# Output pieces sent in turn from SyncE and GpSimd, with a buffer for each, and the first piece scaled in column halves

## The chip, the cores and the metric

The kernel runs on one core of a Trainium2 chip. The metric is the device time of one execution in microseconds. The profile is of one execution; its times count from the start of its span.

## The reference

Two layers follow each other. The first is a linear-attention recurrence over r, k and v (batch 4, heads 8, sequence 768, head size 48). Its output, read as x with 3072 rows and 384 columns, goes into a soft mixture of experts with 32 slots (8 experts, 4 slots each):

```python
logits = x @ phi                         # 3072 x 32
d = softmax(logits over rows)            # dispatch
slot_input = d.T @ x                     # 32 x 384
for e in range(E):
    slot_out[e] = relu(slot_input[e] @ w1[e]) @ w2[e]
c = softmax(logits over slots)           # combine
return (c @ slot_out).astype(np.float32) # 3072 x 384, 4.72 MB
```

Only the last line matters here: every output row is a weighted sum of the 32 rows of slot_out, divided by the sum of its weights.

## The kernel before, in words

The order of the instructions on every engine is written out by hand. The kernel has three parts.

The attention part (to about 97 us of the span) works in twelve steps of 256 rows, two chunks of 128 each. It loads r, k and v through SyncE and forms x and the exponentials of the logits. The exponentials are turned round into `LexpT` (slots on the partitions, one column a row), and their sums over the slots are inverted into `rsum_r`, one value for each row. While it runs, GpSimd scales r and k and issues the loads of all the weights, `w_all`, `w_h` and `w_tail` (`w1_load`, `w2_load`), which convert from float32 to bf16 on the way. An early load, `phi_f` (L116), is GpSimd's too.

The expert part runs from about 97 to 110 us. It ends in two PSUM tiles `sr_p[0]` and `sr_p[1]` of 192 columns (HD) each, which hold slot_out, repeated for four groups of 32 slots. DVE (L726) scales the first into columns 0 to 191 of `so_r`, and ACT (L727) the second into columns 192 to 383.

The output part (L729 to L751) is what the change rewrites. The output is cut into twelve pieces, i = 0 to 11, of 256 rows: 128 partitions with two rows (j = 0, 1) of 384 float32 values, which lie one behind the other in HBM, so that a partition sends 3072 bytes. For each j, two matmuls of 384 columns (q2 = 0, 1) put 64 rows each into one PSUM tile `o_p`. Then j = 0 is scaled by `rsum_r` on DVE (L745) and j = 1 on ACT (L747), both into the SBUF tile `o_s`. Piece 0 leaves in two DMAs, one for each j (L749); every other piece leaves in one DMA of 384 KB (L751). All of them are issued by SyncE. The pool `ob` has six `o_s` buffers, so piece 6 can't be scaled before piece 0 has landed. The pool `out_ps` has four names of `o_p` with two buffers each[...].

At the end of the program (L777) each engine drains, SyncE waits for the DMAs, and the engines meet.

Of the kernel before, what the change touches and what calls it, by code (L numbers as in the profile page):

```python
# [11 lines left out]
def kernel(  # L12
# [12 lines left out]
    nc = tc.nc  # L25
# [3 lines left out]
    Nn, Dm = out.shape  # L29
    assert Nn == B * S and Dm == H * D  # L30
    ES = moe_phi.shape[1]
# [6 lines left out]
    f32 = mybir.dt.float32  # L38
    bf = mybir.dt.bfloat16
    AF = mybir.ActivationFunctionType  # L40
    ALU = mybir.AluOpType

    P = 128
# [9 lines left out]
    HF = P // J  # L53
# [45 lines left out]
    for par in range(2):  # L99
        nc.scalar.dma_start(out=w_pd[par * 64:par * 64 + D, :],  # L100
                            in_=w.rearrange("(q a) d -> a d q", a=2)[par])
# [76 lines left out]
    LexpT = cst.tile([P, nG, P], bf, name="LexpT")  # L178
# [31 lines left out]
    with tc.tile_pool(name="wk", bufs=2) as wk, \  # L210
# [23 lines left out]
        for Wt, ex in ((W_k, ex_k), (W_n, ex_n)):  # L234
            for j in range(J):
                nc.scalar.activation(out=Wt[:, j, :, :].rearrange("p h d -> p (h d)"), in_=lw_p[:], func=AF.Exp,
                                     scale=ex[:, j:j + 1])
# [380 lines left out]
    with tc.tile_pool(name="ffn", bufs=2) as ffn, \  # L618
# [84 lines left out]
        so_r = cst.tile([P, Dm], bf, name="so_r")  # L703
        HD = Dm // 2
# [22 lines left out]
        nc.scalar.activation(out=so_r[:, HD:Dm], in_=sr_p[1][:], func=AF.Copy, scale=csum_c[:])  # L727

    out_ap = out.rearrange("(i p j) m -> i p j m", p=P, j=J)  # L729
    with tc.tile_pool(name="ob", bufs=6) as ob, \  # L730
         tc.tile_pool(name="out_ps", bufs=2, space=bass.MemoryType.PSUM) as out_ps:
        for i in range(nS):
            g, qh = divmod(i, 2)
            o_s = ob.tile([P, J, Dm], f32, name="o_s")
            for j in range(J):
                o_p = out_ps.tile([P, Dm], f32, name=f"o_p{2 * qh + j}")
                for q2 in range(2):
                    q = 2 * qh + q2
                    nc.tensor.matmul(o_p[q2 * HF:(q2 + 1) * HF, :],
                                     LexpT[q * ES:(q + 1) * ES, g, j * HF:(j + 1) * HF],  # L740
                                     so_r[q * ES:(q + 1) * ES, :],
                                     tile_position=(q * ES, q2 * HF), skip_group_check=True)
                sc_col = rsum_r[:, g * G + 2 * j + qh:g * G + 2 * j + qh + 1]
                if j == 0:
                    nc.vector.tensor_scalar_mul(o_s[:, j, :], o_p[:], sc_col)  # L745
                else:
                    nc.scalar.activation(out=o_s[:, j, :], in_=o_p[:], func=AF.Copy, scale=sc_col)  # L747
                if i == 0:
                    nc.sync.dma_start(out=out_ap[i][:, j, :], in_=o_s[:, j, :])  # L749
            if i > 0:  # L750
                nc.sync.dma_start(out=out_ap[i], in_=o_s[:])  # L751


# [28 lines left out]
```

## Time and profile before

| | |
|---|---|
| time, median of 5 runs | 129.59 us (128.57 to 133.58) |
| the profiled execution's own time | 128.61 us |
| its span | 126.4 us, granted TensorE clock 0.91 |
| busy in the span | PE 96.8 us, DVE 92.4, ACT 79.1, POOL 77.7 |
| output DMAs | 11 of 384 KB, median 4.6 us from issue to landing, and 2 of 192 KB, 2.9 us |
| HBM | 39.38 MB read, 4.72 MB written |

The span goes from the first to the last instruction; the rest of an execution's time lies around it. A busy share is an average over the three parts; what a change in the output part is worth has to be read in the last 17 us.

### The profile page before, as it was taken

The numbers are of one execution on the slowest core, as the hardware profiler recorded it, in microseconds if no ns is written. First come the engines' busy times: TensorE is split into PE (matmuls) and PEld (weight loads), VectorE is DVE, ScalarE is ACT, GpSimd is POOL, SyncE is SP. The second block draws the span as 40 slices with busy tenths as digits, with TensorE's granted clock in tenths as the row PEclk, the third lists the DMA queues.
The fourth block names the chain that finished last, engine by engine and source line by source line (L and its number), as shares of the span: only waits on it lengthen the run. The fifth ranks groups of instructions, "written<-read, shape, count | busy, mean of one in ns | idle before, by whom it ended". The sixth has DMA issues, their size and how long they took to land.

```text
span 126.4 us, 4177 instructions
## 1 busy us (share of the span) xinstructions
PE 96.8 (77%) x1779; PEld 69.6 (55%) x1779; DVE 92.4 (73%) x180; ACT 79.1 (63%) x143; POOL 77.7 (61%) x70
## 2 busy tenths in 40 slices
PE   3994799968697888269698959979699999794100
PEld 3483578756566666157485738767576566521000
DVE  5499989999999999275999995999963421284700
ACT  5869495969697966278688877779422320283600
POOL 6008999899998899998599999997420000000000
PEclk9999999999999999756999995899999999995555
DMA  3999999999999999999999999999999999069992
GB/s 77 302 324 325 325 328 267 325 212 232 282 296 290 229 260 256 344 252 301 236 255 257 242 213 220 218 215 214 217 218 213 216 201 180 16 249 365 395 399 93
DMA packets 23544, 31.78 MB, mean 251 GB/s; under 512 B 10451, under 2 KB 18133, under 8 KB 23525
## 3 DMA queue, kind: packets, MB, share of 16 engines
q0 software_dynamic: 4816, 12.63, 51.3%
q1 hardware_dynamic: 18288, 18.88, 47.6%
q8 instruction: 14, 0.23, 0.7%
q10 hardware_dynamic: 420, 0.00, 0.2%
q14 instruction: 6, 0.04, 0.1%
HBM read 39.38 MB, written 4.72 MB: 349 GB/s over the span
## 4 chain that ended last, share of the span: by engine, by line
DMA 45%; PE 14%; POOL 12%; SPq 8%; ACT 6%; DVE 6%; issue 4%; POOLq 0%; DVEq 0%; ACTq 0%
DMA w_tail<-in_moe_w_dram 15%; DMA rkv<-in_v_dram 14%; DMA w_h<-in_moe_w_dram 10%; SPq L83 8%; DMA out_dram<-o_s 6%; POOL kk L256 3%; PE t_p L312 3%; POOL rkv L257 3%; POOL rr L254 3%; PE aat_p L331 2%; PE s_p L382 2%; DVE at_s L343 2%; ACT t_kk L319 2%; DVE rpun L294 2%; PE lw_p L232 1%
## 5 line engine op out<-in xcount | busy, mean ns | idle before, releaser
L343 DVE TENSOR_TENSOR at_s<-aat_p,mask 128x512 bf16<-128x512 f32 x47 | 30.2, 684 | 4.2 <-PE aat_p L331 3.9
L254 POOL TENSOR_TENSOR rr<-rkv,W_n 128x768 bf16<-128x768 f32 x11 | 20.1, 1825 | 10.2 <-DMA rkv<-in_r_dram 10.1
L257 POOL TENSOR_TENSOR rkv<-rkv,u_rep 128x768 f32<-128x768 f32 x11 | 19.9, 1810 | 0.9
L256 POOL TENSOR_TENSOR kk<-rkv,W_k 128x768 bf16<-128x768 f32 x11 | 20.0, 1817 | 0.1
L331 PE MATMUL aat_p<-t_rr,t_kk 64*64 64x128 bf16 x376 | 12.0, 243 | 9.2 <-ACT t_kk L319 6.6
L277 ACT COPY rpun<-rkv 128x384 f32<-128x384 f32 x23 | 11.3, 492 | 9.6 <-PE rpun L491 7.5
L331 PEld LDWEIGHTS <-t_kk 64*64 64x64 bf16 x384 | 8.4, 119 | 12.4 <-ACT t_kk L319 8.7
L301 DVE TENSOR_TENSOR dv<-v_bf,rpun 128x768 bf16<-128x768 bf16 x12 | 11.4, 954 | 3.6 <-ACT v_bf L264 2.6
L319 ACT COPY t_kk<-t_p 128x1024 bf16<-128x1024 bf16 x12 | 12.2, 1013 | 1.4 <-PE t_p L312 1.4
L283 DVE TENSOR_TENSOR rkv<-rkv,rpun 128x384 f32<-128x384 f32 x23 | 12.6, 548 | 0.1
L294 DVE TENSOR_REDUCE rpun<-rkv 128x16 f32<-128x768 f32 x12 | 11.5, 961 | 0.4
L264 ACT CAST v_bf<-rkv 128x768 bf16<-128x768 f32 x12 | 10.0, 831 | 2.9 <-DMA rkv<-in_v_dram 2.9
L319 ACT COPY t_rr<-t_p 128x1024 bf16<-128x1024 bf16 x11 | 11.2, 1016 | 0.5 <-PE t_p L312 0.3
L382 PE MATMUL s_p<-v_bf,kk 64*128 64x96 bf16 x160 | 11.4, 218 | 0.0
L391 DVE TENSOR_TENSOR st<-s_p,wm 128x384 bf16<-128x384 f32 x20 | 10.9, 547 | 0.5 <-PE s_p L382 0.3
L433 ACT COPY xt_s<-xl_p 128x768 bf16<-128x768 bf16 x11 | 8.8, 798 | 3.4 <-PE xl_p L431 3.3
L382 PEld LDWEIGHTS <-kk 64*128 64x128 bf16 x160 | 8.3, 102 | 3.8 <-issue 3.7
L745 DVE TENSOR_SCALAR o_s<-o_p,rsum_r 128x384 f32<-128x384 f32 x12 | 7.0, 615 | 3.7 <-DMA out_dram<-o_s 3.2
L412 ACT CAST x_t<-y_p 128x384 bf16<-128x384 f32 x22 | 9.6, 494 | 0.0
L312 PE MATMUL t_p<-ident,kk 128*128 128x128 bf16 x96 | 8.3, 234 | 1.2 <-ACT Lexp L478 0.6
L488 PE MATMUL rpun<-Lexp,x_t 128*128 128x32 bf16 x66 | 5.2, 180 | 5.2 <-DVE dv L301 5.1
L747 ACT ACTIVATE o_s<-o_p,rsum_r 128x384 f32<-128x384 f32 x12 | 6.4, 584 | 4.1 <-DMA out_dram<-o_s 3.5
(130 smaller groups left out, 186.3 us busy)
## 6 DMA issues: line engine op xcount, KB each, us to landing
w_all<-in_moe_w_dram POOLq DMA_DIRECT2D x8, 768.0 KB, 11.7
out_dram<-o_s SPq DMA_DIRECT2D x11, 384.0 KB, 4.6
w_h<-in_moe_w_dram POOLq DMA_DIRECT2D x4, 768.0 KB, 12.4
w_tail<-in_moe_w_dram POOLq DMA_DIRECT2D x3, 768.0 KB, 18.9
rkv<-in_k_dram SPq DMA_DIRECT2D x3, 384.0 KB, 4.5
rkv<-in_r_dram SPq DMA_DIRECT2D x3, 384.0 KB, 4.9
rkv<-in_v_dram SPq DMA_DIRECT2D x3, 384.0 KB, 5.0
w_tail<-in_moe_w_dram POOLq DMA_DIRECT2D x4, 192.0 KB, 20.1
```

The lines of the kernel that those rows point to most:

```text
L254: nc.gpsimd.tensor_mul(rr[:, :, :, 0:D], r_l, W_n[:])
L256: nc.gpsimd.tensor_mul(kk[:, :, :, 0:D], k_l, W_k[:])
L257: nc.gpsimd.tensor_mul(ku, ku, u_b)
L277: nc.scalar.copy(rp, loads[n][0][:, j, :, :])
L283: nc.vector.tensor_mul(s["ku"][:, j, :, :], s["ku"][:, j, :, :], s["rps"][j])
L294: nc.vector.tensor_reduce(d, s["ku"], axis=mybir.AxisListType.X, op=ALU.add)
L301: nc.vector.tensor_mul(dv[:], s["v"][:], d[:, :, :, None].to_broadcast([P, J, H, D]))
L312: nc.tensor.transpose(t_p[:, q, :, j, :], s[nm][:, j, 2 * q:2 * q + 2, :].rearrange("p h d -> p (h d)"), ident[:])
L319: nc.scalar.copy(t_s[:], s.pop("p_" + nm)[:])
L331: nc.tensor.matmul(at_p[a][g * HF:(g + 1) * HF, q, :], kT[sl, q, g, j, :], rT[sl, q, g, :, :].rearrange("p j c -> p (j c)"), start=True, s ...
L343: nc.vector.tensor_mul(s["at"][:, a, j, :, :], at_p[a][:], mask[:, j, None, :].to_broadcast([P, nP, P]))
L382: nc.tensor.matmul(s_p[:, q * D2:(q + 1) * D2], s["kk"][sl, j, 2 * q:2 * q + 2, :].rearrange("p h d -> p (h d)"), s["v"][sl, j, 2 * q:2 * ...
```

## The change

It touches the output loop alone.

- The pool `ob` has twelve buffers, one for each piece.
- The DMAs of pieces 2, 4, 6, 8 and 10 are issued by SyncE as before; those of pieces 1, 3, 5, 7, 9 and 11 by GpSimd. Of piece 0, the row j = 0 is issued by SyncE and j = 1 by GpSimd.
- Piece 0 is computed in column halves: for each j, columns 0 to 191 go through one `o_p` and DVE, columns 192 to 383 through another `o_p` and ACT. Before, DVE scaled the whole of j = 0 and ACT the whole of j = 1.

```diff
-    with tc.tile_pool(name="ob", bufs=6) as ob, \
+    with tc.tile_pool(name="ob", bufs=12) as ob, \
          tc.tile_pool(name="out_ps", bufs=2, space=bass.MemoryType.PSUM) as out_ps:
         for i in range(nS):
             g, qh = divmod(i, 2)
             o_s = ob.tile([P, J, Dm], f32, name="o_s")
+            put = nc.sync.dma_start if i % 2 == 0 else nc.gpsimd.dma_start
             for j in range(J):
-                o_p = out_ps.tile([P, Dm], f32, name=f"o_p{2 * qh + j}")
-                for q2 in range(2):
-                    q = 2 * qh + q2
-                    nc.tensor.matmul(o_p[q2 * HF:(q2 + 1) * HF, :],
-                                     LexpT[q * ES:(q + 1) * ES, g, j * HF:(j + 1) * HF],
-                                     so_r[q * ES:(q + 1) * ES, :],
-                                     tile_position=(q * ES, q2 * HF), skip_group_check=True)
                 sc_col = rsum_r[:, g * G + 2 * j + qh:g * G + 2 * j + qh + 1]
-                if j == 0:
-                    nc.vector.tensor_scalar_mul(o_s[:, j, :], o_p[:], sc_col)
-                else:
-                    nc.scalar.activation(out=o_s[:, j, :], in_=o_p[:], func=AF.Copy, scale=sc_col)
+                parts = ((0, HD), (HD, Dm)) if i == 0 else ((0, Dm),)
+                for c, (d0, d1) in enumerate(parts):
+                    o_p = out_ps.tile([P, Dm], f32, name=f"o_p{2 * j + c if i == 0 else 2 * qh + j}")
+                    for q2 in range(2):
+                        q = 2 * qh + q2
+                        nc.tensor.matmul(o_p[q2 * HF:(q2 + 1) * HF, d0:d1],
+                                         LexpT[q * ES:(q + 1) * ES, g, j * HF:(j + 1) * HF],
+                                         so_r[q * ES:(q + 1) * ES, d0:d1],
+                                         tile_position=(q * ES, q2 * HF), skip_group_check=True)
+                    if (c if i == 0 else j) == 0:
+                        nc.vector.tensor_scalar_mul(o_s[:, j, d0:d1], o_p[:, d0:d1], sc_col)
+                    else:
+                        nc.scalar.activation(out=o_s[:, j, d0:d1], in_=o_p[:, d0:d1], func=AF.Copy, scale=sc_col)
                 if i == 0:
-                    nc.sync.dma_start(out=out_ap[i][:, j, :], in_=o_s[:, j, :])
+                    (nc.sync if j == 0 else nc.gpsimd).dma_start(out=out_ap[i][:, j, :], in_=o_s[:, j, :])
             if i > 0:
-                nc.sync.dma_start(out=out_ap[i], in_=o_s[:])
+                put(out=out_ap[i], in_=o_s[:])
```

## The prediction

> **What bounds the kernel now.** I read the page first (the 40 slices and the chain that ended last), then the chain in order of time, the windows of the last 16 us, each SyncE issue there, the DMA view in narrow windows, and the closing instructions. The change touches nothing before 109.6 us of the span, so the question is only what sets the time from there to 126.4 us.
>
> The chain of waits, its last steps (start, length, what):
>
> ```profile
> 109.26 0.43 ACT so_r L727
> 109.73 0.61 PE o_p L739 x8
> 110.34 0.90 ACT o_s L747 x2
> 111.24 3.67 DMA out_dram<-o_s
> 115.09 4.45 DMA out_dram<-o_s
> ```
>
> The chain runs through output DMAs. The windows tell whether that is their latency or their volume (length; busy us of PE, PEld, DVE, ACT, POOL; granted clock; DMA share; GB/s):
>
> ```profile
> 111.40:111.60 0.20, 0.20 (x4) 0.14 (x4) 0.20 (x1) 0.20 (x1) 0.00 (x0) 1.00 0.00 0
> 111.60:112.00 0.40, 0.39 (x6) 0.10 (x4) 0.40 (x2) 0.40 (x2) 0.00 (x0) 1.00 0.74 261
> 112.00:114.60 2.60, 1.94 (x16) 0.43 (x16) 1.42 (x3) 1.26 (x3) 0.00 (x0) 0.86 1.04 386
> 114.70:115.00 0.30, 0.00 (x0) 0.00 (x0) 0.00 (x0) 0.00 (x0) 0.00 (x0) 0.50 0.21 72
> 115.00:124.00 9.00, 1.70 (x8) 0.36 (x7) 3.71 (x6) 3.48 (x6) 0.00 (x0) 0.50 1.01 394
> 124.00:125.20 1.20, 0.00 (x0) 0.00 (x0) 0.00 (x0) 0.00 (x0) 0.00 (x0) 0.50 0.06 23
> ```
>
> It is volume. From about 111.66 us the 16 DMA engines are full at 386 to 394 GB/s until 124.0. 4.72 MB at 394 GB/s take 11.97 us; 12.3 pass. The only hole is 114.7 to 115.0, worth 0.3 x (1 - 0.21) = 0.24 us. After 124.0 a share of 0.06 is one engine of sixteen: a straggler that works to nearly 125.2. POOL is idle here.
>
> What made the hole? Two SyncE issues, from narrow timelines:
>
> ```profile
> 110.82 0.37 SPq L749 DMA_DIRECT2D out_dram<-o_s  x1
> 112.81 1.69 SPq L751 DMA_DIRECT2D out_dram<-o_s  x1
> ```
>
> DVE and ACT had filled all six buffers by 113.42, without a wait. SyncE held one issue for 1.69 us, to 114.50, and piece 3's bytes came about 0.5 us later. So the hole is an issue held back on SyncE's queue, not a missing buffer. The waits of L745 and L747 for output DMAs (3.2 and 3.5 us in all) lie beside full DMA engines.
>
> **Part 1, twelve buffers.** They remove these waits: six scaled pieces at 0.62 us follow at once, so scaling ends near 118 instead of 120.3. Bytes leave no sooner, since the DMA engines are full: 0 us. Twice the buffers where six served: 0.
>
> **Part 2, column halves on piece 0.** Four matmuls of 384 columns become eight of 192, with four weight loads more; the scaling becomes two instructions of 128x192 side by side for each j. The nearest rows are L726 and L727 (128x192 out of PSUM, 0.42 us each, writing bf16), against 0.62 and 0.58 for 128x384.
> - Before: o_p from 109.73, DVE from 110.18 to 110.80, SyncE issues at 110.82, bytes at 111.66 (0.84 later).
> - After: the first half needs only DVE's half of so_r, ready at 109.60 against 109.68, and its matmuls are half as long: DVE from about 110.05, ACT from 110.15, both done by 110.57. SyncE issues at 110.60, bytes at 111.44. Gain 0.22 us; between 0.1 (no earlier start) and 0.3.
> - j=1: DVE from 110.5, ACT from 110.6, done at 111.02. It is free for issue at 111.05, 0.19 earlier than SyncE issued it before (111.24).
>
> **Part 3, every other piece to GpSimd.** SyncE keeps the first half-piece and pieces 2, 4, 6, 8, 10; GpSimd gets the second half-piece and 1, 3, 5, 7, 9, 11. GpSimd issues in 0.53 to 0.59 us (L194, 128 rows each), 7 x 0.56 = 3.9 us on an idle engine: its issuing costs nothing. Nothing is queued behind it but the closing drain. What counts is when its first bytes move. The trace of before has no store from GpSimd, but it has a load from an idle GpSimd, phi_f at 2.01 us (L116, issue 0.92). DMA view, window 2.9 to 4.8, then 4.8 to 5.7 (packets, MB, share):
>
> ```profile
> q0 software_dynamic: 1, 0.00, 0.4%
> q0 software_dynamic: 31, 0.05, 14.3%
> ```
>
> All but one of its 32 packets moved after 4.8: 2.8 us after its issue began, 1.9 after it ended. The w_all load issued at 35.43 beside busy GpSimd work is later still; window 35.5 to 39.8:
>
> ```profile
> q0 software_dynamic: 2, 0.00, 0.5%
> ```
>
> That is over 4.3 us. Against it stands the Trainium skill, "DMA: Bandwidth & Descriptors", section "Latency and other measured facts": about 1 us to the first byte by GpSimd's path, 0.6 by SyncE's. By the rule the second half-piece, issued at 111.05, has bytes at 112.05, 0.1 us after the first half-piece (0.197 MB, 0.50 us, to 111.94) is through. By the row, 2.8 less the 0.36 by which this issue is shorter, they come at 113.5. I take the row. Bounds: 112.05 and 115.4.
>
> Then SyncE's next piece comes first. Scaling: piece 1 done at 111.63, piece 2 at 112.22, issue 112.25, bytes at 113.11. **So from 111.94 to 113.11 nothing moves: 1.17 us.** Before, SyncE alone had the second half-piece and piece 1 on their way (issues 111.24 and 111.78), with no gap. After 113.11, piece 2 lasts to 114.11; GpSimd's one and a half pieces (113.5 and 114.1) and piece 4 (114.35) join before that, and there is no second hole. The remaining 11.5 pieces at 1.00 us (0.393 MB at 394 GB/s) end at 124.6 instead of 124.0: **+0.6 us**. The earlier start (0.22) and the closed hole (0.24) are already in it. With the rule: 111.44 + 0.1 + 11.97 = 123.5, -0.5 us.
>
> A second rule bears on this: "SBUF — State Buffer", section "SBUF: two separate sides", the "DVE blocks DMA" trap: while VectorE runs in a two-port mode, GpSimd can't write its descriptors. VectorE is busy to 118 without a break, so a lock would keep the first GpSimd bytes back to about 118, and SyncE's issues would have to carry the stream. L745 takes 617 ns for 384 columns, 1.6 ns each, and reads PSUM; the same page ties the trap to SBUF-to-SBUF work. I take 0.
>
> **The ends.** (a) The straggler. Before, one engine finishes 1.2 us after the rest. Its lag is early: the second half-piece landed at 114.91, 3.67 us after its issue, the first after 2.2; an instruction packet of 16 KB (q8) moves in the window 112.5 to 112.8. The new gap lets such an engine catch up in part: between 0 and -0.9 us, I take -0.4. (b) The close. SyncE's last wait ends near 125.2 and its drain comes at 125.6, 0.4 later. GpSimd's own:
>
> ```profile
> L777 POOLq DRAIN  x3: 51/102/18527, 91.0 to 126.1; - x3
> ```
>
> The 18.53 us one, begun at 91.0, ends at 109.5; the last w_tail load landed at 108.69 (90.23 + 18.46). If that drain waits for GpSimd's transfers, it ends 0.85 us after the last of them, 0.45 worse than SyncE's way. Piece 11 is GpSimd's, so I take +0.4 (0 to +0.5).
>
> **Sum**: +0.6 - 0.4 + 0.4 = +0.6 us. The profiled execution's 128.61 (span 126.4 and 2.2 around it) becomes 129.2. It lay 1.0 below the median of the runs, 129.59; against that median I forecast 129.59 + 0.6 = **130.2 us**. About 1%, 1.3 us, is what a measurement of this kernel can tell from no change.
>
> **Rivals.**
> - *GpSimd's first byte is quick and the straggler vanishes* (faster). -0.5 by the rule, -0.9 without the straggler, and a close that costs nothing: -1.4, 128.2. For it: the straggler is real time, and two queues let fifteen engines run on while one blocks SyncE's issue. Against: no row has GpSimd's bytes within 2.8 us. Chance 0.14.
> - *GpSimd's queue becomes the bound* (slower). Place: the making of descriptors. The weight loads can't show its pace, for they were queued behind others (landings of 18.9 us). If each transfer occupies the maker for the 1.94 us that phi_f took after its issue, the seventh transfer's bytes start at 113.5 + 6 x 1.94 = 125.1, move until 126.1 and land some 0.3 later, near 126.4 against 125.2: +1.2, with the close +1.6; with 4.3 us to the first byte (115.4) instead of 2.4, +3.5. It decides from about 1.75 us a transfer, where the seventh would start later than 124.0. Between the two: +2.1, 131.7. For it: the late first bytes; against: issues of 0.52 us apart fed a full queue. Chance 0.34.
> - *The change does what it says and it is hidden*: the gap, the straggler and the drain stay within 1.3 us of before. That is the forecast. Chance 0.52.
>
> **Range.** The likeliest case alone spans 129.0 to 131.0. Down to 128.5 it takes in most of the faster case, up to 132.0 the slower one up to its middle: 128.5 to 132.0. Chances: faster by over 1% 0.14, within 0.52, slower 0.34.
>
> **What would show it.** Right: SyncE's first issue near 110.6; an empty DMA stretch of about 1 us from 112; software packets from 113 to 114; no o_s wait on DMA; no hole near 114.8; a GpSimd drain 0.8 us after the last landing. Wrong: software packets by 112.2 (then faster), or software packets alone and thin behind 124 (then slower), or a last straggler of over 1.5 us.

## The result, and the profile after

In the first comparison the change made no difference that can be told from none. Over 44 runs its median was 128.92 us (127.83 to 133.10), that of the kernel before 129.18 us over 79 runs. The ratio of the two, taken without the executions that lie over 1.5% above the fastest of their kernel, is 0.9988 with a 95% interval of 0.9971 to 1.0005, which is -0.15 us (-0.37 to +0.06). A second comparison (22 runs against 75, told below) gave 1.0035 (1.0003 to 1.0067), +0.45 us. The forecast of 130.2 us, 0.6 above the median before, lies above the first interval and within the second; the median, 128.92, is inside the range of 128.5 to 132.0.

In the profiled execution of the changed kernel (128.24 us, span 126.4) `so_r` was ready at 109.00 us instead of 109.68, although nothing ahead of it had changed. So I compare the output part from the end of `so_r`. It took 16.73 us before and 17.36 after, 0.63 more. Windows of the changed kernel, to be read as those of before (length; busy us of PE, PEld, DVE, ACT, POOL; granted clock; DMA share; GB/s):

```profile
110.70:111.30 0.60, 0.59 (x9) 0.17 (x8) 0.60 (x2) 0.60 (x2) 0.53 (x1) 1.00 0.85 290
111.30:111.85 0.55, 0.54 (x6) 0.16 (x8) 0.55 (x2) 0.55 (x2) 0.54 (x2) 1.00 0.27 80
111.85:112.40 0.55, 0.53 (x6) 0.15 (x8) 0.55 (x2) 0.55 (x2) 0.14 (x2) 1.00 0.87 316
112.40:123.70 11.30, 1.96 (x16) 0.45 (x15) 3.54 (x7) 3.00 (x7) 2.59 (x5) 0.65 1.01 384
123.70:124.50 0.80, 0.00 (x0) 0.00 (x0) 0.00 (x0) 0.00 (x0) 0.00 (x0) 0.50 0.05 19
```

The first row is the first half-piece; its bytes start at 110.80, 1.8 us after `so_r` instead of 2.0. The second row is the gap: 0.55 us at a share of 0.27. From the third row the engines are full, with no second hole. The bulk, the stretch in which they are full, ends near 123.7. The last row is about one engine alone, as before: the straggler is still there. The last landing, the moment at which the last output DMA reports its end, is 15.53 us after `so_r`; before it was 15.50.

The chain of waits of the changed kernel no longer runs through output DMAs:

```profile
109.05 0.36 PE o_p L743 x3
109.42 5.47 DVE o_s L748 x11
...
115.98 0.49 issue
116.46 0.56 POOLq L780
```

Scaling runs through without a wait and ends in GpSimd's closing drain. The closing instructions (count, shortest/median/longest ns, first and last start):

```profile
L780 POOLq DRAIN  x3: 46/93/9128, 116.5 to 126.1; - x3
L780 SPq DRAIN  x3: 7/7/7, 124.9 to 125.8; - x3
```

GpSimd's drain begins at 116.5 and lasts 9.13 us, to 125.6. SyncE was ready to close at 124.9. The last landing was at 124.5, so the close, from the last landing to the end of the span, takes 1.83 us instead of 1.23.

### The profile page after: what moved, and what is told of

Read it like the earlier page. It is cut to its first block, busy times and chain, and to the rows that moved or that the text cites. A ratio compares the mean times of both kernels' runs of the same rounds, so it can differ in the third digit from the quotient of the medians.

```text
span 126.4 us, 4165 instructions
## 1 busy us (share of the span) xinstructions
PE 97.1 (77%) x1783; PEld 70.1 (55%) x1783; DVE 91.7 (73%) x181; ACT 78.3 (62%) x144; POOL 81.5 (65%) x77
## 4 chain that ended last, share of the span: by engine, by line
DMA 33%; POOL 20%; DVE 15%; PE 10%; SPq 9%; issue 2%; ACT 2%; POOLq 1%; DVEq 0%
DMA w_tail<-in_moe_w_dram 14%; DMA w_h<-in_moe_w_dram 11%; DMA rkv<-in_r_dram 8%; SPq L75 7%; POOL kk L256 6%; POOL rr L254 6%; POOL rkv L257 5%; DVE o_s L748 5%; DVE at_s L343 3%; PE t_p L312 2%; DVE rpun L294 2%; DVE dv L301 2%; PE xl_p L431 2%; POOL w_all L187 2%; DVE rkv L283 2%
## 5 line engine op out<-in xcount | busy, mean ns | idle before, releaser
L752 POOL DMA_DIRECT2D out_dram<-o_s x1 | 0.6, 552 | 18.6 <-ACT o_s L750 18.6
L312 PE MATMUL t_p<-ident,rr 128*128 128x128 bf16 x88 | 8.9, 262 | 0.0
```

The source lines that it names most:

```text
L312: nc.tensor.transpose(t_p[:, q, :, j, :], s[nm][:, j, 2 * q:2 * q + 2, :].rearrange("p h d -> p (h d)"), ident[:])
```

## The experiments

All ratios below are to the kernel before on the same chip. Times after `so_r` come from the one profiled execution of each kernel. In them `so_r` is ready anywhere from 109 to 113 us, which is why only times counted from `so_r` are compared.

### Which queue, and when: the changed kernel taken apart

**All on SyncE** (twelve buffers and halves kept):

```diff
-            put = nc.sync.dma_start if i % 2 == 0 else nc.gpsimd.dma_start
+            put = nc.sync.dma_start
...
-                    (nc.sync if j == 0 else nc.gpsimd).dma_start(...)
+                    nc.sync.dma_start(...)
```

> The changed kernel with every output DMA issued by SyncE; twelve buffers and the column halves stay. Ledger theory (each cost read in the profile after counts in the time: start 0.2 us earlier, a gap of 0.5 us after the first half-piece, a close of GpSimd's drain 0.65 us later than SyncE's, and something before the output part that makes up for it): only the earlier start is left, so 0.2 us under before, ratio 0.998, no gap, close 0.4 us after the last landing. Rival (the close and the gap of the profile do not count in the timed runs, the halves are worth nothing): ratio 1.000.

Measured: 0.9953 (0.9895 to 1.0011). The interval holds both expectations. The profile shows that "no gap" was wrong. The first bytes came at 1.8 us, but SyncE held one issue for 1.91 us and the stream broke for longer than in the kernel before:

```profile
112.25:114.50 2.25, 2.21 (x18) 0.69 (x20) 2.25 (x5) 2.25 (x6) 0.00 (x0) 0.81 0.94 338
114.50:115.40 0.90, 0.90 (x12) 0.23 (x7) 0.90 (x3) 0.90 (x4) 0.00 (x0) 0.50 0.09 26
```

0.9 us at a share of 0.09: that is the hole of before, larger. The last landing was at 15.66.

**GpSimd early only**: the second half of piece 0 and pieces 1, 3 and 5 from GpSimd, the rest from SyncE.

```diff
-            put = nc.sync.dma_start if i % 2 == 0 else nc.gpsimd.dma_start
+            put = nc.gpsimd.dma_start if i in (1, 3, 5) else nc.sync.dma_start
```

> The changed kernel with GpSimd issuing only the second half of piece 0 and pieces 1, 3 and 5; SyncE issues 2, 4 and all from 6 on. Ledger theory: GpSimd's drain ends long before the last landing, so the close is SyncE's again, 0.65 us less than the changed kernel: ratio to before 0.994. Rival (the drain hides behind something else, or costs only under the profiler): as the changed kernel, 0.999.

Measured: 0.9924 (0.9875 to 0.9974), -1.0 us, clear of no change. The drain row of this kernel:

```profile
L780 POOLq DRAIN  x3: 46/102/6845, 114.4 to 126.4; - x3
```

It now ends at 121.2, before the last landing (125.7), and the close takes 0.98 us instead of 1.83. The output part is 16.59 us, 0.77 shorter than in the changed kernel, with the same gap after the first half-piece. Against the kernel before that explains only 0.4 of the 1.0 us: the output part is 0.14 shorter, and the time outside the span 0.26 (1.83 against 2.09, means of these runs). The rest is open. These are six runs, and a near relative of this kernel (1, 3 and 5 alone, below) came out at 0.9976 over 22.

**GpSimd for the last piece only**: as all on SyncE, but piece 11 from GpSimd.

> The kernel e1 with one difference: the last piece, 11, is issued by GpSimd. It prices the close alone. Ledger theory: GpSimd's drain ends 0.9 to 1.1 us after the last landing and the time is 0.6 us above e1, ratio to before 1.003. Rival: no difference from e1 within 0.2 us.

Measured: 0.9985 (0.9926 to 1.0044), 0.4 us above all-on-SyncE, an interval too wide to decide. It did not price the close either. GpSimd issued piece 11 at 118.09 while SyncE had a backlog; the piece overtook that backlog, landed at 122.7, and the drain ended at 123.6, long before the end. But it shows something else: when GpSimd's first bytes move if the engines are full. Its DMA view in the windows 118.1 to 120.25 and 120.25 to 120.6 (packets, MB, share of 16 engines):

```profile
q1 hardware_dynamic: 302, 0.83, 101.7%
...
q0 software_dynamic: 20, 0.12, 88.6%
```

In the first window not one software packet moves; in the second they fill the engines. So the first bytes came 2.2 us after the issue. In the changed kernel, where the engines had run idle, they came 1.1 us after it (issue 110.77, first packet 111.88).

**Both halves of piece 0 on SyncE**, the rest as in the change:

> The changed kernel with both halves of piece 0 issued by SyncE; GpSimd issues 1, 3, 5, 7, 9 and 11. It prices the gap after the first half-piece. Ledger theory: no idle stretch of the DMA engines after the first half, 0.5 us under the changed kernel, ratio to before 0.995. Rival (a straggling DMA engine sets the end, so that the gap is made up later): as the changed kernel, 0.999.

Measured: 0.9998 (0.9955 to 1.0042), the rival's side, against 0.9988 for the change. The gap after the first half-piece was gone, but a smaller one came behind the second:

```profile
115.95:116.30 0.35, 0.35 (x4) 0.07 (x4) 0.35 (x2) 0.35 (x2) 0.00 (x0) 1.00 0.42 149
```

That is 0.35 x (1 - 0.42) = 0.20 us lost, where the change lost 0.55 x (1 - 0.27) = 0.40. The bulk ended 14.45 us after `so_r` instead of 14.69, but the last landing came at 15.30 against 15.53 and GpSimd's drain still closed the program 1.7 us behind it.

### The other two parts alone, and the change once more

These ran together on one chip.

> The changed kernel once more, for a second profile. In the first, the output part (from the end of so_r to the end of the span) was 17.36 us against 16.73 before, and so_r was ready 0.68 us earlier, though nothing ahead of it was changed. Theory that the early so_r is scatter between executions: so_r ends anywhere from 109 to 110.5 here, and the output part is again 17.2 to 17.5. Rival (the output part scatters, and was long in that one execution): the output part comes out near 16.7. Ratio to before 0.999 in either case.

Measured: 1.0035 (1.0003 to 1.0067). Of its profile: output part 17.07 us, last landing 15.50, close 1.57. So both theories have a part: the output part scatters by 0.3 us between two executions, and the end of `so_r` by more. On this chip the spans average 126.94 us for the change and 126.35 before, +0.6, while the time outside the span is 1.82 against 2.04 (means of the runs that the ratio uses).

**Twelve buffers alone** (`bufs=6` to `bufs=12` in the kernel before):

> The kernel before with twelve output buffers instead of six; one queue, no halves. Prediction's step (the buffer waits lie beside full DMA engines): no change, ratio 1.000 within 0.003, scaling ends near 8 us after so_r, SyncE still holds one issue for 1.5 to 2 us. Rival (the buffers feed SyncE's queue and close the hole): 0.3 us less, 0.998.

Measured: 1.0001 (0.9969 to 1.0033). The bulk ended 14.01 us after `so_r` instead of 14.3, with hardly a hole (the longest held issue was 1.21 us, shorter than I expected), and the last landing stayed at 15.54, the output part at 16.75. The stream got smoother and the time did not move. The rival had the hole right and its price wrong: the last landing does not follow the bulk here.

**The change without the halves** (piece 0 scaled by rows):

```diff
-                parts = ((0, HD), (HD, Dm)) if i == 0 else ((0, Dm),)
+                parts = ((0, Dm),)
...
-                    if (c if i == 0 else j) == 0:
+                    if j == 0:
```

> The changed kernel with piece 0 scaled as before (row j = 0 on DVE, j = 1 on ACT), two queues and twelve buffers as in the change. Ledger theory: the first bytes 0.2 us later than in the changed kernel (2.0 after so_r instead of 1.8), GpSimd's share no later, so 0 to 0.2 us over it: ratio to before 1.000. Rival (halves cost more in instructions than they bring): 0.2 us under it, 0.997.

Measured: 1.0039 (1.0011 to 1.0067), next to 1.0035 for the change on the same chip. First bytes at 2.0 instead of 1.8, as expected; the time can't tell 0.2 us. Its last landing, 16.5, is the latest of all.

**GpSimd for 1, 3 and 5 alone**, both halves on SyncE:

> SyncE issues both halves of piece 0, pieces 2 and 4 and all from 6 on; GpSimd only 1, 3 and 5. It takes away the gap after the first half-piece and GpSimd's drain at the end. Ledger theory: 0.2 to 0.3 us under the kernel with the late pieces alone moved back (0.9924), ratio to before 0.990. Rival (the second queue fills what one leaves, so the order of the first pieces doesn't count): 0.992 to 0.994.

Measured: 0.9976 (0.9945 to 1.0008). Output part 16.34, the shortest so far, with the last landing again at 15.42. The interval takes in 0.9945 and so reaches neither the 0.990 that I expected nor the rival's 0.992 to 0.994. On the same chip the change has 1.0035: this kernel is 0.6% (0.8 us) below it, with intervals that just overlap (0.9945 to 1.0008 and 1.0003 to 1.0067). Its close is 0.92 us, where the change's is 1.57.

### What the last landing waits for

Ten profiles had last landings of 15.3 to 15.7 us after `so_r` (one 16.5), while their bulk ended anywhere from 14.0 to 14.9. One thing was common to all of them. The DMA view of the kernel before, window 112.3 to 113.8, has beside the output this row:

```profile
q8 instruction: 1, 0.02, 4.0%
```

That is one packet of 16 KB, and 4.0% of sixteen engines for 1.5 us is 0.96 us on one engine, the time of a whole output piece. It begins 2.3 to 2.9 us after `so_r` in all ten, each time when TensorE has reached about the same place of its program. The one landing of 16.5 goes with the longest of these packets, 1.64 us; the other nine took 0.97 to 1.43. The page of the kernel before has 14 of them in the span:

```profile
q8 instruction: 14, 0.23, 0.7%
```

That is one for each 256 of TensorE's 3558 instructions (1779 matmuls and as many weight loads). The Trainium skill describes them ("Runtime: NRT & Kernel Launch", section "Instruction fetch mechanics"): an engine's instructions are refilled in blocks of 16 KiB, 256 instructions, over DMA, at a cost that it calls mostly hidden. The size and the spacing agree with this trace; that it is hidden had to be tried.

The next three kernels cut each of 23 filler matmuls of 384 columns (nothing uses their results) into two of 192. With each matmul goes a weight load, so that puts 46 more instructions ahead of the output, and it changes nothing in the output. The place at which the block is asked for then lies ahead of the output's stream.

```diff
-            for _ in range(count):
-                nc.tensor.matmul(pad[:], ident[:], w1_all[:, 0, 0, 0:Dm],
+            for _ in range(2 * count):
+                nc.tensor.matmul(pad[:, 0:Dm // 2], ident[:], w1_all[:, 0, 0, 0:Dm // 2],
```

(in `fill` and in `keep`).

> The kernel before, with each of the 23 filler matmuls of 384 columns[...] cut into two of 192 (46 TensorE instructions more, hardly more columns time). In every profile so far one 16 KB instruction packet (q8) begins 2.5 to 2.9 us after so_r, when TensorE has reached the same place of its program, and keeps one DMA engine for about 1 us in the middle of the output; with 46 instructions more ahead of it that place is reached near so_r, in the 2 us in which the DMA engines stand idle. Straggler theory (that packet is why the last landing is 15.3 to 15.6 us after so_r in all nine profiles whatever the stream did): the packet comes 0 to 0.6 us after so_r, no hole from a held SyncE issue, last landing 14.5 to 14.8, 0.8 us less time, ratio to before 0.994. Rival (the straggling engine is slow for another reason, and the volume sets the end): last landing still 15.3 to 15.6, ratio 1.000 to 1.003.

Measured: 0.9917 (0.9883 to 0.9951), -1.1 us. The packet moved to 108.0 us, 0.9 us ahead of the end of `so_r` (I had expected 0 to 0.6 us behind it), into idle DMA engines. Its DMA view, window 107.9 to 109.3:

```profile
q8 instruction: 1, 0.02, 4.9%
```

And the output, windows of the bulk and behind it:

```profile
110.90:122.90 12.00, 3.97 (x26) 0.92 (x23) 5.38 (x10) 5.03 (x10) 0.00 (x0) 0.57 1.02 393
122.90:123.50 0.60, 0.00 (x0) 0.00 (x0) 0.00 (x0) 0.00 (x0) 0.00 (x0) 0.50 0.03 10
```

No hole, the bulk ends 14.05 us after `so_r`, and the last landing at 14.64 instead of 15.50. The held issue is gone too. The row of SyncE's output issues (shortest/median/longest ns), first before, then here:

```profile
L751 SPq DMA_DIRECT2D out_dram<-o_s x11: 379/881/1687, 111.8 to 120.6; - x11
```

```profile
L751 SPq DMA_DIRECT2D out_dram<-o_s x11: 379/881/1010, 111.0 to 119.4; - x11
```

Nothing in the output part of the program differs between the two kernels, so the place of the packet is what moved the last landing. The pair of kernels with 1, 3 and 5 alone on GpSimd, below, repeats it (15.42 to 14.82). So the cost of a block was not hidden here. The landing gives 0.86 of the 1.1 us; the rest is within the interval. The hole and the held issue went with the packet in this profile, but twelve buffers had made the hole nearly vanish with the packet in place. The likely way, which no view shows (the trace does not name the engine of a packet), is that the engine that fetches the block falls behind, and that SyncE's queue can't take the next transfer until that engine has caught up.

> The changed kernel with the same 23 filler matmuls cut in two. Straggler theory: without the straggler the gap after the first half-piece counts, the bulk ends 14.6 to 14.7 us after so_r and the last landing is 0.3 later, 14.9 to 15.0, with GpSimd's close 1.6 behind it: 0.5 us under the changed kernel, but 0.5 to 0.8 us over the kernel before with the cut fillers. Rival (the straggler is not the packet): last landing 15.5 as in the changed kernel, no difference from it.

Measured: 0.9993 (0.9955 to 1.0031) on the same chip. Against the kernel before with the cut fillers that is 0.9993 / 0.9917 = 1.008, 1.0 us slower, and the two intervals do not meet. The bulk ended at 14.75, the gap is as wide as in the change, the drain closed 1.7 us behind the last landing. That landing, 15.35, is later than the 14.9 to 15.0 that I expected, because I had put 0.3 us between the end of the bulk and the last landing. It is 0.6 here, and 0.6 too in the kernel before with the cut fillers (14.05 and 14.64). So with the packet out of the way the landing follows the bulk, and the costs of the change count: 0.71 us at the landing and 0.5 at the close (1.72 against 1.23), less 0.3 outside the span (1.80 against 2.11), make 0.9 of the measured 1.0 us.

> The kernel e8 (GpSimd issues pieces 1, 3 and 5 alone) with the same 23 filler matmuls cut in two. Straggler theory: first bytes at 1.8, bulk end 14.2, last landing 14.5, close 0.9: output part 15.4 instead of 16.3, 0.9 us under e8, ratio to before 0.990. Rival: last landing 15.4 as in e8, ratio 0.9976.

Measured: 0.9920 (0.9889 to 0.9952). Last landing 14.82, output part 15.72, 0.62 under the same kernel without the cut fillers, where I had expected 0.9.

**The version that the experiments point to**: the kernel before, with the cut fillers and the column halves, nothing else of the change.

> The kernel before with the cut fillers (as e9) and with the column halves of piece 0 alone from the change: six buffers, every output DMA issued by SyncE. If the end is set by the volume of the output once the 16 KB packet is out of the way, the 0.2 us by which the halves start the stream earlier comes through whole: first bytes 1.8 us after so_r, last landing 14.4 to 14.5, output part 15.65 against 15.87 in e9, ratio to before 0.990. Rival (something else still sets the end, or another packet falls into the stream): last landing 14.6 or later, ratio 0.992 or more, no gain on e9.

Measured: 0.9866 (0.9817 to 0.9915), the lowest ratio of all (six runs, median 127.70 us). First bytes at 1.8, bulk to 13.8, last landing 14.44, output part 15.68: within 0.04 us of what was expected. That it beats the kernel without halves in time (0.9917, another chip) is not shown, for the intervals meet.

## Why the prediction was wrong, point by point

**The steps that failed.** The sum put +0.2 us at the last landing (+0.6 for the gap, -0.4 for the straggler), +0.4 at the close and nothing outside the span. Measured in the two profiles were +0.03 and 0.00 at the landing and +0.6 and +0.34 at the close, and outside the span -0.2 us (means of the second comparison). The gap was mis-sized by two ("I take the row"), what was left of it was hidden behind the straggler, and the 2.2 us around the span were carried over without a reason. With 0.2 outside, the terms of the first profile make 0.03 + 0.6 - 0.2 = +0.4, which is what the second comparison shows (+0.45). The first shows -0.15; no run explains that difference. Of the distance between 130.2 and the measured 128.92, 0.4 us is the starting point: the median of five runs, 129.59, lay above that of 79, 129.18.

**The bound** was right in kind and incomplete. The output part is DMA volume; but its end was set by what a block of TensorE's instructions held up. I had that in hand as "a straggler", with its packet in the next sentence, and did not take it for the bound.

**Part 1, twelve buffers, 0 us**: right, 1.0001. Scaling without waits ended 6.9 us after `so_r`, where the forecast of 118 us meant 8.3; six pieces at 0.62 from 113.42 would have given 117.1 by its own numbers. That a missing buffer did not make the hole holds: with twelve buffers and all on SyncE it was larger (0.9 us), and with six and the packet moved it was gone. Why it was hardly there with twelve buffers alone stays open.

**Part 2, the halves, -0.22**: the size is right, -0.21 (1.79 against 2.00 after `so_r`). In the change it was lost behind the straggler. In the last kernel the landing moves by 0.20 with it.

**Part 3, the gap, 1.17 us**: mis-sized by two; it was 0.55. The failed step is "I take the row". The row of phi_f, 2.8 us to the first bytes, was that of a load issued while SyncE's loads filled the engines, as the DMA view of the kernel before has beside it (window 2.9 to 4.8):

```profile
q1 hardware_dynamic: 1540, 0.58, 110.9%
```

What the row measured was, in all likelihood, mostly that queue. With idle engines the first bytes come after 1.1 us, as the rule said, and with full ones after 2.2 us. The rule alone, though, forecast a gap of 0.1. Most of the rest is GpSimd's late start, 0.4 us, which the step "its issuing costs nothing" left out. The second half-piece was ready 1.2 us after `so_r` but GpSimd issued it at 1.77, where I had 1.37. GpSimd's output issues in the changed kernel begin 0.54 to 0.63 us after their piece is scaled, SyncE's 0.03 to 0.07. The end of the chain above shows it for the last piece: scaled at 115.95, then 0.49 us of "issue" before GpSimd's DMA. On the other side, scaled pieces follow each other at 0.53 us from start to start, where I took the duration of 0.62, so SyncE issued piece 2 at 2.28 instead of 2.57. Bulk end: +0.4 instead of +0.6.

**The ends.** The straggler: I took -0.4, and the last landing moved by +0.03 against a bulk end 0.4 later, so -0.4 it was. But the reason was not that the gap lets the engine catch up: without that gap (both halves on SyncE) the last landing was 15.30, and in nine of ten profiles it was 15.3 to 15.7 wherever the bulk ended between 14.0 and 14.9. So a shift of the bulk by less than the straggler's lag was free, in the change too. The close: +0.4 forecast, +0.6 and +0.34 measured. The drain does wait for GpSimd's transfers. It ends 1.1 us after the last landing, and in the kernels where GpSimd stops early (121.2 us with 1, 3 and 5) it ends early too.

**The sum** was +0.6 in the span. The first profile has +0.63 from `so_r` to the end, the second +0.34, and the mean spans of the second comparison +0.6. That it agrees is in part luck: the landing rose by less than forecast and the close by more. What the sum left out is the time outside the span, 2.2 us in the profile before and 1.9 after. In the kernel before, the trace has one packet more, behind the end of its span (window 126.4 to 131):

```profile
q14 instruction: 1, 0.01, 0.7%
```

The change has none. Of all twelve experiments, those with at least 12 output DMAs issued by SyncE have this packet and 1.9 to 2.2 us outside the span (means of their runs); those with at most 10 do not have it and have 1.8 us. So some 0.2 us may come back because SyncE issues less. The kernels agree in it, but no experiment was made for it, and the cause is not shown.

What stays open is the 0.6 us between the two comparisons. Their intervals just overlap, and the scatter of the time at which `so_r` is ready, 109 to 111 us in twelve of the fourteen profiles, is larger than either.

**The rivals.** The faster one ("quick first byte and the straggler vanishes") had the first half right and the second wrong: the second queue did not free the straggler, and the close was not free. The slower one ("GpSimd's queue becomes the bound") is refuted: from 112.4 us on the engines are full at a share of 1.01. The third, that the costs stay within 1.3 us of before, is what came, though with other sizes.

## What to carry to other kernels

When a stage is bound by DMA volume, look at what its last landing waits for, not at its bulk: one engine of sixteen that is late hides losses and gains on the others up to its own lag. Here the lag went with the place of one block of instructions, and 46 small instructions more, ahead of the stage, gave 1.1 us where the change with two queues, twice the buffers and an earlier start gave nothing. Issue the last transfers of a kernel from SyncE if GpSimd's drain would close behind them (the close took 1.83 and 1.57 us in the change, 0.98 and 0.92 with the late pieces on SyncE), and before taking a latency from a row, see what stood in the queue at that moment.

## What the runs showed of the hardware

- A block of TensorE's instructions (16 KB, q8) took one DMA engine 0.97 us in the output of the kernel before, and up to 1.64 in others: as long as one 384 KB piece takes all sixteen, or longer. Moved out of the output stream, it gave 0.86 us at the last landing and 1.1 us in time.
- SyncE's longest output issue took 1.69 us before, 1.91 with all on SyncE and halves, and 1.01 with the packet moved.
- GpSimd's first bytes moved 1.1 us after the start of the issue with idle engines, 2.2 us with full ones; SyncE's 0.86 with idle ones (issued 0.93 us after `so_r`, first bytes at 1.79).
- In the profile's rows GpSimd began its output issues about 0.55 us after the piece was scaled, SyncE 0.03 to 0.07 when nothing was queued ahead (changed kernel). The change without halves is an exception: there GpSimd's first issue, which waits for ACT alone, began after 0.30.
- GpSimd's closing drain ended 0.9 to 1.2 us after the last of its own output transfers had landed (13.02 and 12.11 us after `so_r` with piece 11 alone, 16.59 and 15.43 in the change).
- Two transfers issued together need not move together. In the changed kernel, piece 1 (GpSimd, issued at 111.33) moved only behind piece 2 (SyncE, issued at 111.28). Its bytes began about 2.1 us after its issue, near the 2.2 us that GpSimd needed on full engines, so that this wait may be the whole reason. DMA views of the windows 112.5 to 113.4 and 113.5 to 114.5:

```profile
q1 hardware_dynamic: 104, 0.32, 93.5%
q0 software_dynamic: 10, 0.02, 10.9%
```

```profile
q0 software_dynamic: 55, 0.32, 85.8%
q1 hardware_dynamic: 15, 0.02, 6.5%
```

- VectorE's scaling out of PSUM, busy without a break, did not hold back GpSimd's first bytes: they came 1.1 us after the issue.
